# A gated mix of full and local attention on one core: projections, folds and spare matmuls on 32-column strips, local products moved to GpSimd

## The chip, the cores and the metric

One NeuronCore of a Trainium2 chip runs the whole kernel; the other cores are idle. The metric is the device time of one execution in microseconds (us). In this text PE is TensorE, ACT is ScalarE, DVE is VectorE, POOL is GpSimd and SP is SyncE, the names that the profile uses.

## The reference

Two attentions over the same input, mixed by a gate for each position, in bfloat16:

```python
x = A_x                                       # 1 x 2048 x 640, 32 heads of 20
g = sigmoid((x * gate_w).sum(-1, keepdims=True))
a = full attention: q, k, v = split(x @ A_wqkv); softmax(q @ k.T * 20**-0.5) @ v; @ A_wo
b = local attention: q, k, v = split(x @ B_wqkv); position s looks at s, s-2, ..., s-14
    (8 positions, those below 0 masked), softmax over the 8, weighted sum of v; @ B_wo
out = g * a + (1 - g) * b
```

The full attention has 32 x 2048 x 2048 exponentials, and that is where the time goes.

## The kernel before, in words

**Units and steps.** The scores are cut into units of 128 keys x 512 queries of one head: 4 chunks of queries x 8 quads of heads x 16 blocks of keys x 4 heads of a quad = 2048 units. A group is one chunk and one quad (64 units). A step is what ScalarE exponentiates with one instruction (`mk_exp`, L1377): two or three units that lie side by side in PSUM, in banks 0 to 2 and 3 to 4 by turns, where bank 5 joins the second when it is free. TensorE makes the scores of a step in `mk_qk` (L1319; heads are 32 rows of the array each), and multiplies the exponentials with the values in `mk_pv` (L1411; the output of each of four heads is a strip of 32 columns of the array, so four run side by side). Bank 6 gathers a group's sum; when it is done, `gen_norm` transposes and divides it on VectorE.

**Units of VectorE.** Some units never reach ScalarE. The lanes `gen_xm`, `gen_xr` and `gen_x` take a unit into bank 5 or 7, or in place of the third unit of a step (`xstep`, which has to meet a deadline with a margin, `XMARG`). VectorE copies it out as scaled 16-bit integers (L1566), and for every two units three instructions (L1596, L1600, L1604) make two bfloat16 parts of the exponential out of the bits. Both parts go to L1411, so that such a unit costs TensorE two of its matmuls.

**Projections and folds.** `gen_k`, `gen_q`, `gen_v`, `gen_F` and `gen_V` project x to keys, queries and values through `chain` and `mm_part` (L503) and `v_chunk` (L614), with matmuls of 128 x 128 weights; `q_fin` (L714) adds a bound that takes the place of the softmax's maximum. `gen_fold` and `gen_prefold` multiply the finished attention outputs by the output weights, also by L503, and `a_half` (L862) and `l_pre` (L896) do so at the end. `spare` (L1914, L1919, L1929) puts matmuls without use into idle time of TensorE: it does so when the planner's share of busy time in the last 3413 ns falls below `SPW`.

**The local attention.** For each of 4 chunks of 512 positions: `gen_F` makes q and k, multiplies them on VectorE (L1016) and sums over a head with a matmul against `Sel` (L992, strips of 32 columns). `gen_K` makes the softmax over the 8 positions on VectorE, and then, for each block of 128 positions, TensorE transposes the weights into strips, VectorE copies them to `attnT` (L1123), and four products of two window positions each follow on VectorE, 1280 elements for each partition. The first (L1150) writes to `accs`; the other three (L1160) write to one of `NTM` = 2 buffers `tmps`, and each is added to `accs` by two accumulating DMAs, one for each window position, which GpSimd issues (L1162). The second buffers of both kinds lie in parts of x that are dead by then (`xT`). When all have landed, VectorE adds the two halves of `accs` (L1177), and the fold of the chunk can take them.

**What sets the order.** The order of instructions on every engine is fixed when the kernel is built. A planner (`_Sched.task` and the loop at the end of `_build`) keeps a clock for every engine, with a cost for every instruction, and emits steps one after the other; between two steps it asks the lanes (`ready`) whether their next instruction fits before TensorE's next scores are due. 20 constants steer it, `BASE_`, or an entry of `SEG` for each stretch of 24 steps: among them `SPW`, `XMARG`, the least number of units that a group keeps for the other lanes, and `LW`, the local work that VectorE ought to have done by the end. On the chip each engine runs its own list in order and waits with semaphores where a task depends on another engine's.

Of the kernel before, what the change touches and what calls it, by code (L numbers as in the profile page):

```python
# [6 lines left out]
BF16 = mybir.dt.bfloat16  # L7
# [43 lines left out]
BASE_ = (0.65, 500.0, 28, 4, 10, 12, 315000.0, 1, 0.0, 1, 1.0, 40, 20, 3000.0, 1e9, 3, 8, 2, -1, 200.0)  # L51
SEG = {
# [51 lines left out]
class _Sched:  # L104
# [6 lines left out]
    def __init__(self, nc, ctx):  # L111
        self.nc = nc
        self.lists = {s: [] for s in self.STREAMS}
        self.sems = {s: ctx.enter_context(nc.semaphore("s_" + s)) for s in self.STREAMS}
        self.dma_sems = {
            s: [ctx.enter_context(nc.semaphore("d_%s%d" % (s, i))) for i in range(n)]
            for s, n in self.DMA_POOL.items()
        }
        self.bufs = {}
        self.n = 0  # L120
        self.dma_final = {}
        self.clk = {s: 0.0 for s in self.STREAMS}
        self.mode = None
        self.flow = []
        self.made = []

    def task(self, stream, fn, reads=(), writes=(), dma=False, accum=(), extra=(), cost=60.0, mode="s", dlat=4000.0, flow=None):
# [34 lines left out]
        if dma:  # L162
            t.end = at + dlat
            t.fin = t.end
            self.clk[stream] = at + (860.0 if stream == "pool" else 500.0)
        else:
            if stream == "pe":
                if mode != self.mode:
                    at += self.TURN
                    self.mode = mode  # L170
                self.flow.append((at, cost if flow is None else flow))
            t.end = at + cost
# [141 lines left out]
def _build(ctx, nc, A_x, A_wqkv, A_wo, B_wqkv, B_wo, gate_w, out):  # L314
# [27 lines left out]
    attnT = sb([P, WIN * P], BF16, "attnT")  # L342
    NPR = 3
# [150 lines left out]

    bst = {b: None for b in SB}

    def mm_part(b, mms, k0, n, reads, cost):
        bst[b] = "mid" if k0 + len(mms) < n else None

        def fn(e):  # L500
            ins = None
            for k, (o, l, r) in enumerate(mms):
                ins = e.matmul(o, l, r, start=(k0 + k == 0), stop=(k0 + k == n - 1))  # L503
            return ins

        if k0 == 0:
            return T("pe", fn, reads=reads, writes=[("bk", b)], cost=cost)
        return T("pe", fn, reads=reads, accum=[("bk", b)], cost=cost)
# [83 lines left out]
    def chain(b, mms, reads, w=1.0, cost=MM):  # L592
        n = len(mms)
        for k, m in enumerate(mms):
            yield ("pe", cost, w)
# [11 lines left out]
    def v_chunk(b, p, gi, kb, i_):  # L607
# [3 lines left out]
        def fn(e):  # L611
            ins = None
            for c in range(CN):
                ins = e.matmul(bank[b][:, i_ * wn:(i_ + 1) * wn], xT[:, kb // 4, c, (kb % 4) * P:(kb % 4 + 1) * P],  # L614
                               WvA[:, c, w0:w0 + wn], start=(c == 0), stop=(c == CN - 1))
# [3 lines left out]
        if i_ == 0:  # L619
            T("pe", fn, reads=rd, writes=[("bk", b)], cost=375)  # L620
        else:
            T("pe", fn, reads=rd, accum=[("bk", b)], cost=375)
# [25 lines left out]
    def gen_v(p, g0=0):  # L648
        for gi in range(g0, 6):
            b = yield from take(True)  # L650
            lo, hi = VG[gi]
            for i_, kb in enumerate(range(lo, hi)):
                yield ("pe", 375.0, 1.0)
# [36 lines left out]
    def gen_q(gi):  # L690
# [12 lines left out]
        yield ("pe", MM, 1.0)  # L703
# [9 lines left out]
    def q_fin(b, gi, q):  # L713
        T("pe", lambda e: e.matmul(bank[b], KM[:, q, :], qabs_hi, start=False, stop=True, skip_group_check=True),  # L714
          reads=["qabs", ("KM", q)], accum=[("bk", b)], cost=MM)
# [39 lines left out]
    def gen_norm(gi):  # L755
# [16 lines left out]
        for a, z in zip(cut, cut[1:]):  # L772
# [3 lines left out]
            if gi < HG:  # L776
                yield ("dve", 170.0 + 1.05 * (z - a) * m, 0.0)
            T("dve", lambda e, rg_v=rg_v, rr_b=rr_b, c=c, w=z - a: e.tensor_tensor(rgD[st][:, mo:mo + m, c:c + w], rg_v, rr_b, ALU.mult),
              reads=["rg", ("rr", i)], writes=[("rgD", st, h) for h in sorted({c // 32, (c + z - a - 1) // 32})], cost=170.0 + 1.05 * (z - a) * m)
# [79 lines left out]
    def a_half(o, blk, hf, fs, first, last, b):  # L859
        for f in fs:  # L860
            st, sp = first and f == fs[0], last and f == fs[-1]
            T("pe", lambda e, f=f, st=st, sp=sp: e.matmul(o, *a_mm(o, QCN - 1, f, blk, FW * hf)[1:], start=st, stop=sp),  # L862
              reads=[("oTh", max(0, blk - 1)) if f == CN - 1 else ("oT", (QCN - 1) % 2, f)] + w_rd(f),
              **({"writes": [("bk", b)]} if st else {"accum": [("bk", b)]}), cost=140)
# [7 lines left out]
    def gen_lfold():  # L872
        for blk in (0, 1, 2):
            for hf in range(2):
# [4 lines left out]
                yield ("pe", 280.0, 1.0)  # L879
# [13 lines left out]
    def l_pre(hf, k):  # L893
        b = l_banks()[hf]
        if k < 2:
            T("pe", lambda e: e.matmul(bank[b][:, 0:FW], ident[:, :], acch[:, k, hf, :], start=(k == 0), stop=False),  # L896
              reads=["ident", ("acch", k, hf)], **({"accum": [("bk", b)]} if k else {"writes": [("bk", b)]}), cost=140)
# [46 lines left out]
    KPC = 1480.0  # L944
    DLAT, DSLACK = 4700.0, 500.0
    tmrd = {}

    def gen_F(tc):
# [33 lines left out]
        for half in range(2):  # L982
# [20 lines left out]
            for idx in range(2 * CN):  # L1003
# [5 lines left out]
                if wq == 1 and f > 0:  # L1009
# [7 lines left out]
                      reads=["qB", "kB"], writes=[("prod", r)], cost=690)  # L1017
# [39 lines left out]
    def gen_K(tc):  # L1057
# [27 lines left out]
        T("dve", lambda e: e.tensor_tensor(M_(4), L_q(0, 4), L_q(4, 4), ALU.max), reads=["L"], writes=["aT"], cost=420)  # L1085
        yield ("dve", 290.0, 290.0)
        T("dve", lambda e: e.tensor_tensor(M_(2), M_(2), M_hi(2), ALU.max), reads=["aT"], writes=["aT"], cost=290)
        yield ("dve", 220.0, 220.0)
        T("dve", lambda e: e.tensor_tensor(mx[:, :, :], M_(1), M_hi(1), ALU.max), reads=["aT"], writes=["mx"], cost=220)
        yield ("dve", 700.0, 700.0)  # L1090
        yield after(T("dve", lambda e: e.tensor_tensor(L_4d, L_4d, mx_b, ALU.subtract), reads=["mx"], writes=["L"], cost=700))
# [6 lines left out]
        T("dve", lambda e: e.tensor_tensor(S_(0, 4), L_q(0, 4), L_q(4, 4), ALU.add), reads=["L"], writes=["aT"], cost=690)  # L1098
        yield ("dve", 430.0, 430.0)
        T("dve", lambda e: e.tensor_tensor(S_(0, 2), S_(0, 2), S_(2, 2), ALU.add), reads=["aT"], writes=["aT"], cost=430)  # L1100
        yield ("dve", 290.0, 290.0)
        T("dve", lambda e: e.tensor_tensor(sm[:, :, :], S_(0, 1), S_(1, 1), ALU.add), reads=["aT"], writes=["sm"], cost=290)
# [4 lines left out]
        T("dve", lambda e, gBb=gBb: e.tensor_tensor(sm[:, :, :], sm[:, :, :], gBb, ALU.mult), reads=["gB"], writes=["sm"], cost=280)  # L1107
        T("dve", lambda e: e.tensor_tensor(A_4d, A_4d, sm_b, ALU.mult), reads=["sm"], writes=["L"], cost=1225)
# [990 lines left out]
```

## Time and profile before

| what | value |
|---|---|
| median of 3 runs | 864.42 us (864.2 to 864.7) |
| the profiled execution | 865.48 us, of which the span from first to last instruction is 863.7 |
| mean granted TensorE clock | 0.987 |
| instructions | 16606; TensorE 6862 matmuls and as many weight loads |
| busy | TensorE 798.3 us, VectorE 716.9, ScalarE 839.3, GpSimd 87.3 |
| exponentials on ScalarE (L1377) | 755 instructions, 826.3 us |
| units on VectorE (L1566) | 232 |
| local products on VectorE (L1150, L1160) | 16 and 48, about 1.48 us each |
| accumulating DMAs issued by GpSimd (L1162) | 96, 84.2 us; 3.7 to 4.5 us to landing |

A row of the page's groups reads: line, engine, operation, output <- input, count | busy time, mean length of one in ns | idle time of the engine just before, and what ended it. A row of the stretches table reads: stretch, its length, then for PE, PEld (weight loads), DVE, ACT and POOL the busy time and in brackets the number of instructions, then the granted clock, the share of the DMA engines and GB/s. A row of a timeline reads: start, length, engine, line, operation, names, count, and in square brackets the idle time ahead of it and who ended that.

### The profile page before, as it was taken

The page shows a single profiled execution, that of the slowest core. Times are in us where ns is not written, and L with a number is a line of the kernel's source. Part 1 is how long each engine was busy: PE and PEld are TensorE (multiplying, and loading weights), DVE is VectorE, ACT ScalarE, POOL GpSimd, SP SyncE. Part 2 cuts the span into 40 slices and gives each one's busy share as a digit, 9 for nine tenths or more (in the row PEclk, how much of TensorE's full clock was granted, in tenths as well). Part 3 has the DMA queues.
Part 4 walks back from the last instruction along what each step waited for, and adds up shares of the span by engine and source line. Part 5 has one row for each costly group of instructions (what it writes and reads, how often), then busy time and mean ns, then how long its engine had stood idle before and what let it go on. Part 6 is the DMA issues. An engine that isn't in the chain of part 4 may idle for free.

```text
span 863.7 us, 16606 instructions
## 1 busy us (share of the span) xinstructions
PE 798.3 (92%) x6862; PEld 246.9 (29%) x6862; DVE 716.9 (83%) x1303; ACT 839.3 (97%) x781; POOL 87.3 (10%) x103
## 2 busy tenths in 40 slices
PE   9999999999999999988999999998998999788996
PEld 6322332223333222222232222322122232222233
DVE  6586867878777779888888998998699898999885
ACT  6999999999999999999999999999799999999997
POOL 1000000000000022022222210033020000332000
PEclk9999999999999999999999999999699999999999
DMA  8233011011010175378456631198260011886000
GB/s 184 45 50 52 6 25 8 3 29 8 4 10 6 38 109 105 41 119 128 68 106 98 111 60 38 19 181 127 32 104 5 10 13 25 138 129 108 1 2 32
DMA packets 141311, 51.30 MB, mean 59 GB/s; under 512 B 120628, under 2 KB 128948, under 8 KB 141236
## 3 DMA queue, kind: packets, MB, share of 16 engines
q0 software_dynamic: 13824, 31.46, 21.7%
q1 hardware_dynamic: 126612, 18.59, 14.1%
q8 instruction: 54, 0.88, 0.4%
q10 hardware_dynamic: 800, 0.18, 0.1%
q14 instruction: 21, 0.17, 0.1%
HBM read 16.14 MB, written 2.62 MB: 22 GB/s over the span
## 4 chain that ended last, share of the span: by engine, by line
ACT 84%; DMA 6%; PE 5%; DVE 3%; issue 1%; POOL 0%; SPq 0%; DVEq 0%
ACT ebuf L1377 84%; DMA accW<-tmps 3%; DMA accW<-xT 2%; PE ps L1319 2%; PE ps L503 1%; PE ps L1411 1%; DVE tmps L1160 1%; DVE accW L1150 1%; PE ps L1229 1%; DMA x_tm<-in_A_x_dram 1%; PE ps L1205 0%; ACT L_sb L1093 0%; DVE xt L1566 0%; POOL accW L1162 0%; DVE attnT L1123 0%
## 5 line engine op out<-in xcount | busy, mean ns | idle before, releaser
L1377 ACT ACTIVATE ebuf<-ps 128x1536 bf16<-128x1536 f32 (+1 forms) x755 | 826.3, 1412 | 11.3 <-PE ps L1319 11.3
L1319 PE MATMUL ps<-qT,kT 32*128 32x512 bf16 x1984 | 297.6, 388 | 51.6 <-ACT ebuf L1377 38.5
L1411 PE MATMUL ps<-ebuf,vA 128*21 128x512 bf16 (+2 forms) x1926 | 208.2, 374 | 0.5 <-DVE vA L632 0.4
L1566 DVE TENSOR_SCALAR xt<-ps 128x512 int16<-128x512 f32 x232 | 157.5, 685 | 52.9 <-PE ps L1319 51.2
L1319 PEld LDWEIGHTS ps<-qT,kT 32*128 32x128 bf16 x1984 | 72.0, 91 | 328.0 <-ACT ebuf L1377 281.2
L1162 POOL DMA_DIRECT2D accW<-tmps x36 | 31.6, 952 | 550.5 <-DVE rr L768 311.9
L1604 DVE TENSOR_TENSOR xw<-xt,xw 128x1024 bf16<-128x1024 bf16 x116 | 79.1, 682 | 1.6
L503 PE MATMUL ps<-xT,WqkB 128*128 128x512 bf16 x200 | 62.9, 390 | 1.4 <-DVE lgtr L1022 1.2
L1411 PE MATMUL ps<-xw,vA 128*21 128x512 bf16 (+2 forms) x250 | 64.1, 373 | 0.0
L1411 PEld LDWEIGHTS ps<-ebuf,vA 128*21 128x21 bf16 x1926 | 43.1, 90 | 64.0 <-issue 54.8
L1411 PE MATMUL ps<-xe,vA 128*21 128x512 bf16 (+2 forms) x250 | 59.7, 375 | 0.0
L1016 DVE TENSOR_TENSOR prod<-qk 128x1024 bf16<-128x1024 bf16 x80 | 51.9, 682 | 2.1 <-PE ps L992 1.9
L1600 DVE TENSOR_SCALAR xw<-xt 128x1024 uint16<-128x1024 uint16 x116 | 48.7, 420 | 3.9 <-PE ps L1411 3.7
L1596 DVE TENSOR_SCALAR xe<-xt 128x1024 uint16<-128x1024 uint16 x116 | 48.5, 418 | 2.6 <-PE ps L1411 1.8
L503 PE MATMUL ps<-xT,WqP 128*128 128x512 bf16 x155 | 47.8, 391 | 0.3 <-DVE xt L1566 0.2
L503 PE MATMUL ps<-xT,WkP 128*128 128x512 bf16 x140 | 41.8, 384 | 0.0
L717 DVE TENSOR_SCALAR qT<-ps 128x512 bf16<-128x512 f32 x32 | 22.1, 690 | 16.7 <-PE ps L714 16.6
L503 PE MATMUL ps<-WvA,oBacc 128*128 128x320 bf16 x160 | 32.0, 307 | 1.2 <-DVE outsb L825 1.2
L979 DVE CAST qk<-ps 128x512 bf16<-128x512 f32 x40 | 27.2, 681 | 6.6 <-PE ps L503 6.3
L614 PE MATMUL ps<-WvA,xT 128*128 128x160 bf16 (+1 forms) x320 | 30.6, 234 | 0.0
L503 PE MATMUL ps<-woA_r,oTd 128*128 128x320 bf16 x144 | 29.5, 301 | 0.0
L503 PE MATMUL ps<-xT,WvB 128*128 128x512 bf16 x100 | 29.3, 383 | 0.0
(129 smaller groups left out, 708.3 us busy)
## 6 DMA issues: line engine op xcount, KB each, us to landing
accW<-tmps POOLq DMA_DIRECT2D x36, 320.0 KB, 4.5
accW<-xT POOLq DMA_DIRECT2D x24, 320.0 KB, 4.4
xT<-xT POOLq DMA_DIRECT2D x24, 320.0 KB, 4.2
WqkB<-in_B_wqkv_dram SPq DMA_DIRECT2D x40, 160.0 KB
xT<-tmps POOLq DMA_DIRECT2D x12, 320.0 KB, 3.7
WqP<-in_A_wqkv_dram SPq DMA_DIRECT2D x135, 20.0 KB
x_tm<-in_A_x_dram SPq DMA_DIRECT2D x8, 320.0 KB
out_dram<-outsb SPq DMA_DIRECT2D x24, 80.0 KB
```

The costliest lines, as they stand in the source:

```text
L503: ins = e.matmul(o, l, r, start=(k0 + k == 0), stop=(k0 + k == n - 1))
L614: ins = e.matmul(bank[b][:, i_ * wn:(i_ + 1) * wn], xT[:, kb // 4, c, (kb % 4) * P:(kb % 4 + 1) * P], WvA[:, c, w0:w0 + wn], start=(c == 0 ...
L979: give(b, T("dve", lambda e, dst=dst, b=b: e.tensor_copy(dst, bank[b]), reads=[("bk", b)], writes=[key], cost=690))
L1016: t = T("dve", lambda e, r=r, q_ap=q_ap, k_ap=k_ap: e.tensor_tensor(prod[r][:, :, :], q_ap, k_ap, ALU.mult), reads=["qB", "kB"], writes=[( ...
L1162: tmrd[m] = [T("pool", lambda e, r=r, m=m: e.dma_start(accs[r], tmps[m][:, D * (r % 2):D * (r % 2) + D], accum_op=ALU.add), reads=[("tmps" ...
L1319: return e.matmul(o, kT[js, q, kb * P:(kb + 1) * P], qT[g % NQT][js, :], start=True, stop=True)
L1377: return T("act", lambda e: e.activation(ebuf[:, 512 * p:512 * (p + n)], ps[:, b0 * 512:(b0 + n) * 512], ACTF.Exp, scale=LN2 / ONE), reads ...
L1411: ins = e.matmul(bank[OB][32 * j:32 * j + DH + 1, o:o + w], vv, ap[:, w * i:w * i + w], start=st and i == 0, stop=sp and i == len(ks) - 1)
L1566: r = T("dve", lambda e, b=b, i=i, sl=sl: e.tensor_scalar(xt[sl][:, 512 * i:512 * i + 512].bitcast(I16), bank[b], XB, 0.0, op0=ALU.add, op ...
L1596: tx = T("dve", lambda e, r=r, t0=t0: e.tensor_scalar(xe[r][:, :].bitcast(U16), t0.bitcast(U16), 0x7F80, XMU, op0=ALU.bitwise_and, op1=ALU ...
L1600: T("dve", lambda e, r=r, t0=t0: e.tensor_scalar(xw[r][:, :].bitcast(U16), t0.bitcast(U16), 0x007F, 0x3F00, op0=ALU.bitwise_and, op1=ALU.b ...
L1604: t = T("dve", lambda e, r=r, t0=t0: e.tensor_tensor(xw[r][:, :], t0, xw[r][:, :], ALU.mult), reads=tk, writes=[("xw", r)], cost=690)
```

## The change

It has four parts.

1. *Strips.* A new function issues every matmul of 128 weight columns as four of 32 columns, each into 32 partitions of the same PSUM bank, with the same streamed operand. `mm_part`, `v_chunk`, `q_fin`, `a_half`, `l_pre` and `spare` use it; the planner books them in mode "c", that of L1411. (In the planner a change of mode costs `TURN` = 105 ns.)
2. *Local products.* The four products of a block become eight, one for each window position, 640 elements for each partition, and run on GpSimd. The accumulating DMAs are as before, each issued behind its own half, and the buffer's halves have dependences of their own.
3. *A second buffer of local weights*, `attnU`: blocks take turns, `attns[bl % 2]`. The softmax's scratch use of `attnT` stays.
4. *The planner.* It keeps lists of the last instructions of VectorE and GpSimd that are marked `lock=True`, and starts none of the one engine's within one of the other's: the products on GpSimd, and on VectorE L1016, L1596, L1600, L1604, the rescaling in `gen_norm`, L1177 and the softmax's tensor-tensor instructions. Accumulating DMAs are booked as served one after the other, 1650 ns each, and their issue with 900 ns (860 before). All constants of `BASE_` and `SEG` are other ones (`SPW` mostly 0.6, from 0.65; `XMARG` mostly 80, from 500; `LW` mostly 180000, from 315000), so that everything is placed anew, 258 units as the short description says.

The core of the diff:

```diff
+    attns = [(attnT, "aT"), (sb([P, WIN * P], BF16, "attnU"), "aU")]
...
+    def cols(e, o, l, r, **kw):
+        ins = None
+        for j in range(4):
+            ins = e.matmul(o[32 * j:32 * j + 32, :], l[:, 32 * j:32 * j + 32], r, **kw)
+        return ins
...
     def mm_part(b, mms, k0, n, reads, cost):
...
-                ins = e.matmul(o, l, r, start=(k0 + k == 0), stop=(k0 + k == n - 1))
+                ins = cols(e, o, l, r, start=(k0 + k == 0), stop=(k0 + k == n - 1))
...
-        return T("pe", fn, reads=reads, accum=[("bk", b)], cost=cost)
+        return T("pe", fn, reads=reads, accum=[("bk", b)], cost=cost, mode="c")
...
         def ev_aT(bl, b):
-            return T("dve", lambda e: e.tensor_copy(attnT[:, :], bank_bf[b]), reads=[("bk", b)], writes=["aT"], cost=690)
+            aw, ak = attns[bl % 2]
+            return T("dve", lambda e: e.tensor_copy(aw[:, :], bank_bf[b]), reads=[("bk", b)], writes=[ak], cost=690)
...
-                T("dve", lambda e, vv=vv, av=av, m=m: e.tensor_tensor(tmp4[m], vv, av, ALU.mult),
-                  reads=["aT", vkey], writes=[("tmps", m)] + dead, cost=KPC)
-                tmrd[m] = [T("pool", lambda e, r=r, m=m: e.dma_start(accs[r], tmps[m][:, D * (r % 2):D * (r % 2) + D], accum_op=ALU.add),
-                             reads=[("tmps", m)], writes=[("accs", r)], dma=True, dlat=DLAT) for r in (st, st + 1)]
+                for i in range(2):
+                    av = fap(aw, aw[:, (u + i) * P:(u + i) * P + 1], [[0, CN], [1, P]])
+                    vv = fap(vB4, vB4[:, 0, off + DIL * i:off + DIL * i + 1], [[512 + PADB, CN], [1, P]])
+                    yield ("pool", KPH, KPH)
+                    if u == 0:
+                        T("pool", lambda e, vv=vv, av=av, st=st, i=i: e.tensor_tensor(acc4[st // 2][:, i, :, :], vv, av, ALU.mult),
+                          reads=[ak, vkey], writes=[("accs", st + i)] + dead, cost=KPH, lock=True)
+                        continue
+                    T("pool", lambda e, vv=vv, av=av, m=m, i=i: e.tensor_tensor(tmp4[m][:, i, :, :], vv, av, ALU.mult),
+                      reads=[ak, vkey], writes=[("tmps", m, i)] + dead, cost=KPH, lock=True)
+                    T("pool", lambda e, r=st + i, m=m, i=i: e.dma_start(accs[r], tmps[m][:, D * i:D * i + D], accum_op=ALU.add),
+                      reads=[("tmps", m, i)], writes=[("accs", st + i)], dma=True, dlat=DLAT, serve=1650.0)
...
+        if k == "pool":
+            if clk["pool"] > clk[eng] + 30.0:
+                return False
+            adv(g)
+            return ready(g, s, eng, lim)
...
-        if now + 215.0 + (sch.TURN if sch.mode != "s" else 0.0) > lim or share(now) > SPW:
+        if now + 215.0 + (sch.TURN if sch.mode != "c" else 0.0) > lim or share(now) > SPW:
...
-                T("pe", lambda e, b=b: e.matmul(bank[b], ident[:, :], xT[:, 3, 0, :], start=True, stop=True),
-                  reads=["ident", ("xT", 3)], accum=[("bk", b)], cost=215)
+                T("pe", lambda e, b=b: cols(e, bank[b], ident[:, :], xT[:, 3, 0, :], start=True, stop=True),
+                  reads=["ident", ("xT", 3)], accum=[("bk", b)], cost=215, mode="c")
```

`KPH`, the planner's cost of one product on GpSimd, is 1100 ns; `KPC`, the cost of one of VectorE's, was 1480.

More of the change, by code (lines that the diff above doesn't have):

```diff
@@ L125, in __init__, with task @@
         self.made = []
-    def task(self, stream, fn, reads=(), writes=(), dma=False, accum=(), extra=(), cost=60.0, mode="s", dlat=4000.0, flow=None):
+        self.served = 0.0
+        self.locks = {"dve": [], "pool": []}
+    def task(self, stream, fn, reads=(), writes=(), dma=False, accum=(), extra=(), cost=60.0, mode="s", dlat=4000.0, flow=None, lock=False, serve=0.0):
         deps = {}
@@ L171, in task @@
                 self.flow.append((at, cost if flow is None else flow))
+            if lock:
+                for a, z in self.locks["pool" if stream == "dve" else "dve"]:
+                    if a <= at < z:
+                        at = z
+                self.locks[stream].append((at, at + cost))
+                del self.locks[stream][:-4]
             t.end = at + cost
@@ L619, in v_chunk @@
         if i_ == 0:
-            T("pe", fn, reads=rd, writes=[("bk", b)], cost=375)
+            T("pe", fn, reads=rd, writes=[("bk", b)], cost=375, mode="c")
         else:
-            T("pe", fn, reads=rd, accum=[("bk", b)], cost=375)
+            T("pe", fn, reads=rd, accum=[("bk", b)], cost=375, mode="c")
     def v_evac(b, p, gi, eng="dve"):
@@ L713, in q_fin @@
     def q_fin(b, gi, q):
-        T("pe", lambda e: e.matmul(bank[b], KM[:, q, :], qabs_hi, start=False, stop=True, skip_group_check=True),
-          reads=["qabs", ("KM", q)], accum=[("bk", b)], cost=MM)
+        T("pe", lambda e: cols(e, bank[b], KM[:, q, :], qabs_hi, start=False, stop=True, skip_group_check=True),
+          reads=["qabs", ("KM", q)], accum=[("bk", b)], cost=MM, mode="c")
         qmade.add(gi)
@@ L778, in gen_norm @@
             T("dve", lambda e, rg_v=rg_v, rr_b=rr_b, c=c, w=z - a: e.tensor_tensor(rgD[st][:, mo:mo + m, c:c + w], rg_v, rr_b, ALU.mult),
-              reads=["rg", ("rr", i)], writes=[("rgD", st, h) for h in sorted({c // 32, (c + z - a - 1) // 32})], cost=170.0 + 1.05 * (z - a) * m)
+              reads=["rg", ("rr", i)], writes=[("rgD", st, h) for h in sorted({c // 32, (c + z - a - 1) // 32})], cost=170.0 + 1.05 * (z - a) * m, lock=True)
         for f in range(CN):
@@ L895, in l_pre @@
         if k < 2:
-            T("pe", lambda e: e.matmul(bank[b][:, 0:FW], ident[:, :], acch[:, k, hf, :], start=(k == 0), stop=False),
-              reads=["ident", ("acch", k, hf)], **({"accum": [("bk", b)]} if k else {"writes": [("bk", b)]}), cost=140)
+            T("pe", lambda e: cols(e, bank[b][:, 0:FW], ident[:, :], acch[:, k, hf, :], start=(k == 0), stop=False),
+              reads=["ident", ("acch", k, hf)], **({"accum": [("bk", b)]} if k else {"writes": [("bk", b)]}), cost=140, mode="c")
         else:
@@ L1016, in gen_F @@
                 t = T("dve", lambda e, r=r, q_ap=q_ap, k_ap=k_ap: e.tensor_tensor(prod[r][:, :, :], q_ap, k_ap, ALU.mult),
-                      reads=["qB", "kB"], writes=[("prod", r)], cost=690)
+                      reads=["qB", "kB"], writes=[("prod", r)], cost=690, lock=True)
             yield after(t)
@@ L1148, in gen_K @@
                         dead = [("xT", 1)] if st else []
-                    yield ("dve", KPC, KPC)
-                    T("dve", lambda e, vv=vv, av=av, st=st: e.tensor_tensor(acc4[st // 2], vv, av, ALU.mult),
-                      reads=["aT", vkey], writes=[("accs", st), ("accs", st + 1)] + dead, cost=KPC)
-                    continue
-                m = tmctr[0] % NTM if tc > 0 or dead0() else 0
-                tmctr[0] += 1
-                for t in tmrd.get(m, []):
-                    yield after(t)
@@ L1177, in gen_K @@
                 T("dve", lambda e, acc=acc, fs=fs: e.tensor_tensor(acc, acc3[fs], acc3[fs + 1], ALU.add),
-                  reads=[("accs", fs), ("accs", fs + 1)], writes=[("oBacc", fb)], cost=822)
+                  reads=[("accs", fs), ("accs", fs + 1)], writes=[("oBacc", fb)], cost=822, lock=True)
                 if tc > 0 and bl < 3:
@@ L1597, in gen_x @@
                                                                 op1=ALU.bitwise_or),
-                   reads=tk, writes=[("xe", r)], cost=XTS)
+                   reads=tk, writes=[("xe", r)], cost=XTS, lock=True)
             yield ("dve", XTS, 0.0)
@@ L1601, in gen_x @@
                                                            op1=ALU.bitwise_or),
[L1602 removed]
+              reads=tk, writes=[("xw", r)], cost=XTS, lock=True)
             yield ("dve", 690.0, 0.0)
             t = T("dve", lambda e, r=r, t0=t0: e.tensor_tensor(xw[r][:, :], t0, xw[r][:, :], ALU.mult),
[L1605 removed]
+                  reads=tk, writes=[("xw", r)], cost=690, lock=True)
             xcred[0] -= 1
@@ L1918, in spare @@
         if cnt[0] + xcnt_[0] > 0:
-            T("pe", lambda e: e.matmul(bank[OB], ident[:, :], zrow, start=False, stop=False, skip_group_check=True),
-              reads=["ident", "zt"], accum=[("ob", j) for j in range(4)], cost=215)
+            T("pe", lambda e: cols(e, bank[OB], ident[:, :], zrow, start=False, stop=False, skip_group_check=True),
+              reads=["ident", "zt"], accum=[("ob", j) for j in range(4)], cost=215, mode="c")
             spares[0] += 1
```

70 lines of the change are left out of this document (37 added, 33 removed), and 52 rows, old and new, of the table SEG.

## The prediction

> **What bounds the kernel now.** I read the page's busy table and slices first, then ScalarE's groups with shapes kept apart, the waits, the table by stretches, and last the timelines of VectorE and TensorE around the one stretch where ScalarE falters.
>
> ```profile
> span 863.7 us, 16606 instructions
> ...
> PE 798.3 (92%) x6862; PEld 246.9 (29%) x6862; DVE 716.9 (83%) x1303; ACT 839.3 (97%) x781; POOL 87.3 (10%) x103
> ...
> PEclk9999999999999999999999999999699999999999
> ...
> ACT 84%; DMA 6%; PE 5%; DVE 3%; issue 1%; POOL 0%; SPq 0%; DVEq 0%
> ```
>
> ScalarE is busy 839.3 of 863.7 us. TensorE's 92% are modelled ends of pipelined matmuls; it mostly waits for ScalarE, as the waits show next. The granted clock has one dip.
>
> ```profile
> L1377 ACT ACTIVATE ebuf<-ps 128x1024 bf16<-128x1024 f32 x449 | 512.0, 1240 | 7.9 <-PE ps L1319 7.9
> L1377 ACT ACTIVATE ebuf<-ps 128x1536 bf16<-128x1536 f32 x306 | 509.5, 1665 | 3.4 <-PE ps L1319 3.4
> ...
> PEld ps L1319 <- ACT ebuf L1377: 281.2, 593, 1.4
> ...
> ACT ebuf L1377 <- PE ps L1319: 11.3, 19, 0.9
> ...
> DVE tmps L1160 <- DMA accW<-tmps: 8.2, 6, 2.3
> ```
>
> The first two lines are ScalarE's exponentials: 449 of two score units, 306 of three, so 898 + 918 = 1816 units of the 2048. The missing 232 are the L1566 instructions, where VectorE makes the exponential. Both shapes together are busy 826.3 us (group for line 1377 on the page), 0.455 us a unit at this mix; a third unit in a step adds 1665 - 1240 = 425 ns. ScalarE stands still before exponentials for only 11.3 us. TensorE's score matmuls wait 281.2 us for ScalarE. So the end is set by how many units ScalarE gets, plus its few stalls.
>
> ```profile
> 550.00:600.00 50.00, 46.65 (x428) 13.81 (x424) 45.61 (x71) 50.00 (x46) 13.76 (x16) 1.00 0.74 122
> 600.00:620.00 20.00, 18.55 (x87) 3.22 (x87) 13.81 (x26) 14.44 (x15) 2.08 (x3) 0.57 0.38 66
> ...
> 596.80 0.42 DVE L1600 TENSOR_SCALAR xw<-xt 128x1024 uint16<-128x1024 uint16 x1
> 599.30 1.49 DVE L1160 TENSOR_TENSOR tmps<-vB,attnT 128x1280 f32<-128x1280 bf16 x1 [2.08 <-DMA accW<-tmps]
> 600.71 0.68 DVE L1566 TENSOR_SCALAR xt<-ps 128x512 int16<-128x512 f32 x1
> ...
> 599.23 0.39 PE L1319 MATMUL ps<-qT,kT 32*128 32x512 bf16 x2
> 601.45 0.63 PE L1319 MATMUL ps<-qT,kT 32*128 32x512 bf16 x4 [1.83 <-ACT ebuf L1377]
> ```
>
> These explain half the stalls. At 597.2 VectorE comes to a local product (L1160) whose buffer is still read by an accumulating DMA, and stands for 2.08 us. The copy out of PSUM queued behind it (L1566) is late, TensorE starts nothing from 599.24 to 601.45, its clock falls to 0.57 in the mean over 600 to 620, and ScalarE is busy 14.44 of 20 us, after 50.00 of 50 before. That one wait costs 5.6 us there and 0.2 just after: 5.8 us.
>
> **The change, part by part.** *Units on ScalarE.* I read "258 units placed anew" as VectorE's units, 129 pairs where there are 116. ScalarE then has 26 fewer: 26 x 0.425 = 11.1 us if steps only get narrower, 26 x 0.455 = 11.8 at the same mix; I take **-11.8**. The mix is open: a step costs (826.3 - 1816 x 0.425) / 755 = 0.072 us beside its units; at 2.5 units a step rather than 1816 / 755 = 2.41 there are 28 steps fewer, 2.0 us, and I allow as much the other way.
>
> *Does VectorE have the time?* The local products leave it: 48 of L1160 (70.8 us) and 16 of L1150 (23.8), 94.6 us. A unit costs L1566's 685 ns plus half of L1596, L1600 and L1604 (418 + 420 + 682), 1.445 us; 26 are 37.6 us. VectorE goes from 716.9 to about 660, before any waiting for GpSimd, so the cover is there.
>
> *Products on GpSimd.* 128 halves of 640 elements, and 96 accumulating DMAs as now (36 + 24 + 24 + 12), each for one half. No row shows a GpSimd product. Its nearest rows are IOTA, 160 elements in 270 ns, which gives 1.08 us for 640; below stands half of VectorE's own product, 0.74; above, the strided MEMSET of 512 in 2.44, which gives 3.05. I take 1.1, IOTA's value and also the diff's planning cost; that planner's other costs match their rows (690 for 685, 420 for 418, 1480 for 1478). So 141 us of products, and 84.2 us of DMA issue as now (31.6 + 21.2 + 21.1 + 10.3). The products run in four stretches (308 to 408, 417 to 509, 553 to 645, 724 to 799: 359 us), where GpSimd would be 63% busy; at 1.85 us a product it would be 89%, at 3.05 late by 115 us. Below 1.85 nothing here is on the path.
>
> The Trainium skill ("GPSIMD Engine Reference", Performance versus the Vector engine) gives a two-input operation on 2048 elements as 4497 ns, so 1405 for 640 by estimate. By it the products take 39 us more, still beside other work; no row here shows it.
>
> *Where the stall goes.* The wait for a free product buffer moves to GpSimd's queue. Behind it there stand the next half and its DMA, and who waits for these are VectorE's add L1177, the copy of the local weights two blocks later (two buffers give it that distance), and the fold. VectorE keeps only L1177's wait for DMAs (2.9 us now). The 5.8 us go: **-5.8**. The other stalls, 11.3 - 5.8 - 0.8 at the very first step = 4.7, stay.
>
> *New stalls.* Products on GpSimd now run beside VectorE's instructions and may hold them up, and a static order can be wrong about it. Nothing in this trace prices that: below zero is excluded, since a second reader frees nothing; at the top stands rival A. I take as much as remains, **+4.7**, since VectorE waits for one more in-order partner.
>
> *Strips.* 1417 matmuls (899 on L503, 320 on L614, 32 on L714, 146 spares, 20 in the last fold) become four each: 4251 more matmuls and as many weight loads. Four strips of 512 columns start 219 to 222 ns after the last four (L1411 at 596.38, 596.60, 596.82), a whole one 216 (L503 at 592.515, 592.731, 592.947): 8 ns at most x 1417 = +11 us of TensorE. Projections then have the shape of the L1411 matmuls. A change of shape costs 95 to 100 ns (starts 311 to 317 apart in place of 216), and 165 such changes, counted in the starts, go: -16 us. TensorE gains some 5 us off the path (it has 281 us of waiting): 0. Both ends, +11 and -16, vanish in that wait too. The 8502 instructions more have to be fetched; today's 16606 take queue q8 0.4% of the DMA engines' span (0.88 MB), so I add nothing.
>
> *The planner's constants.* They move work without adding any; the margin ahead of a deadline goes from mostly 500 to 80 ns. That is in the new stalls.
>
> Sum: -11.8 - 5.8 + 4.7 = **-12.9 us**. The profiled execution lies at 865.48 (863.7 span, 1.8 around it), 1.1 above the median of 864.42; from that, **851.5**.
>
> **The rivals.** *A, slower: VectorE and GpSimd hold each other up.* Place: the four local stretches. VectorE is busy 311.8 of 350 us there (windows 320:410, 430:500, 550:640, 700:800), 94% in the last. Each hold-up of VectorE delays L1566 behind it, as at 599. Price: 5.8 us for a gap of 2.2 us on TensorE. For it: a product of 1.1 us is longer than nearly all of VectorE's instructions, and 80 ns of margin covers no collision; POOL's DMA issue already varies, 859 to 1241 ns. Against: the VectorE work that the diff's planner won't place beside a product (its lock lists) is about 297 us (196 for 129 pairs, 52 of L1016, some 49 of small ones), 34% of the span; with products at 141 / 359 = 39% the two fit into 73% even if never together. With one drop per stretch: 851.5 + 4 x 5.8 = 874.7. It decides from the third drop on (two give 863.1, three 868.9). Chance 0.20.
>
> The Trainium skill ("SBUF — State Buffer", Who interferes with whom) states this as an exclusive lock: the instruction that starts second waits for the whole of the first, if VectorE has two SBUF inputs or a two-port mode and GpSimd reads SBUF. By that rule every meeting costs a wait; this trace has no GpSimd product, so no run shows it yet.
>
> *B, more than forecast.* All steady stalls go (10.5 us, not 5.8) and no new ones come: 864.4 - 11.8 - 10.5 = 842.1; 840 with 28 steps fewer. For it: another 1.8 us of ScalarE's stalls (three, 409.5 to 414.8) follow VectorE's waits of 1.40 and 1.31 us at 404.5 and 406.6. Chance 0.18.
>
> *C, the 258 are no new share.* The units stay at 232 and only the stall goes: 864.4 - 5.8 + 4.7 = 863.3. Against: 232 is an even count of pairs, as 258 is, and freed VectorE time asks for use. Chance 0.07 (0.02 faster, 0.04 same, 0.01 slower).
>
> **How the numbers follow.** The forecast has 0.55. Faster: 0.55 + 0.18 + 0.02 = 0.75; same 0.04; slower 0.20 + 0.01 = 0.21. The bound of 0.2%, 1.7 us, is about what a measurement here can tell from no change. The range reaches down to B (840) and up to three clock drops of A (869); some 0.06 lies below and 0.12 above. The forecast's own range is 845 to 858: the mix (2.0) and new stalls from zero to twice 4.7.
>
> **What would show it.** L1566 258 times, and 1790 units in the two shapes of L1377, busy about 814 us; L1160 and L1150 gone from VectorE, 128 products on POOL near 1.1 us; ScalarE's idle before L1377 near 10 us; no clock below 1.00 between 550 and 650; VectorE's products (L1604, L1016) still near 682 ns. Wrong if L1604 or L1566 swell, if PEclk dips in three or more local stretches, if POOL's products pass 1.85 us, or if L1566 counts 232.

## The result, and the profile after

The change makes the kernel slower: 910.54 us (median of 4 runs, 903.8 to 912.88) against 864.31; ratio 1.0522, 95% interval 1.0462 to 1.0583. The profiled execution took 903.8 us, the fastest of the four. In the changed file the exponentials are line 1395 (1377 before), the scores 1337 (1319), VectorE's units 1584 (1566) with 1614, 1618 and 1622 (1596, 1600, 1604), the products for the logits 1032 (1016), the local products 1175 and 1178, their DMAs 1180.

The same rows of the page as before:

```profile
span 902.0 us, 25116 instructions
...
PE 805.3 (89%) x11036; PEld 262.1 (29%) x11037; DVE 769.2 (85%) x1304; ACT 833.7 (92%) x782; POOL 264.3 (29%) x231
...
PEclk9999999999999998989999879989988999896998
...
ACT 60%; DVE 21%; PE 13%; POOL 3%; issue 2%; DMA 1%; POOLq 0%; DVEq 0%
```

ScalarE has less to do, as meant, but VectorE, now without local products, is busy 52 us longer than before, the clock dips again and again from the 16th of the 40 slices on, and 21% of the chain that ended last now runs through VectorE. The groups, shapes kept apart, show where that comes from:

```profile
L1395 ACT ACTIVATE ebuf<-ps 128x1024 bf16<-128x1024 f32 x476 | 505.8, 1173 | 25.2 <-PE ps L1337 24.6
L1395 ACT ACTIVATE ebuf<-ps 128x1536 bf16<-128x1536 f32 x279 | 441.8, 1584 | 30.1 <-PE ps L1337 27.7 <-PE ps L1340 2.3
...
L1584 DVE TENSOR_SCALAR xt<-ps 128x512 int16<-128x512 f32 x258 | 174.5, 684 | 44.4 <-PE ps L1337 41.6 <-PE ps L1340 0.6
L1622 DVE TENSOR_TENSOR xw<-xt,xw 128x1024 bf16<-128x1024 bf16 x129 | 122.7, 951 | 1.9
L1618 DVE TENSOR_SCALAR xw<-xt 128x1024 uint16<-128x1024 uint16 x129 | 77.3, 599 | 8.3 <-PE ps L1429 8.2
L1614 DVE TENSOR_SCALAR xe<-xt 128x1024 uint16<-128x1024 uint16 x129 | 74.5, 578 | 4.6 <-PE ps L1429 3.7
L1032 DVE TENSOR_TENSOR prod<-qk 128x1024 bf16<-128x1024 bf16 x80 | 74.4, 960 | 2.3 <-PE ps L1008 2.1
...
L1178 POOL TENSOR_TENSOR tmps<-vB,attnT 128x640 f32<-128x640 bf16 x16 | 25.9, 1618 | 0.0
```

ScalarE stands still before exponentials for 25.2 and 30.1 us in the two shapes, 55.4 us by the page's group, where it was 11.3. Of VectorE's lines shown, the four that read and write SBUF only have swollen: lines 1622 and 1032 from 682 to 951 and 960 ns, lines 1614 and 1618 from 418 and 420 to 578 and 599. Line 1584, which reads PSUM, has not (684). A product on GpSimd takes 1556 ns in the mean over all 128 (1286 the shortest), not 1100. The stretches table (busy times of PE, PEld, DVE, ACT, POOL, then the granted clock) ties the loss to GpSimd:

```profile
250.00:300.00 50.00, 47.75 (x733) 15.55 (x727) 37.25 (x68) 50.00 (x48) 0.00 (x0) 1.00 0.19 34
...
350.00:400.00 50.00, 41.13 (x445) 10.67 (x443) 46.84 (x61) 41.51 (x38) 26.05 (x23) 0.86 0.52 92
...
650.00:700.00 50.00, 41.20 (x455) 10.10 (x450) 48.63 (x72) 42.25 (x41) 21.95 (x19) 0.90 0.45 66
```

From 20 us to the first product, at 314, ScalarE is busy all the time; in the two stretches with products shown here it loses 8.5 and 7.8 us of 50. The timeline shows one hold-up being passed on:

```profile
347.38 1.60 POOL L1178 TENSOR_TENSOR xT<-vB,attnU 128x640 f32<-128x640 bf16 x1
347.39 2.14 DVE L1032 TENSOR_TENSOR prod<-qk 128x1024 bf16<-128x1024 bf16 x1
...
349.46 2.61 DVE L1622 TENSOR_TENSOR xw<-xt,xw 128x1024 bf16<-128x1024 bf16 x1
...
349.88 1.63 POOL L1178 TENSOR_TENSOR tmps<-vB,attnU 128x640 f32<-128x640 bf16 x1
...
351.99 2.83 DVE L1032 TENSOR_TENSOR prod<-qk 128x1024 bf16<-128x1024 bf16 x2
...
352.66 1.60 POOL L1178 TENSOR_TENSOR tmps<-vB,attnU 128x640 f32<-128x640 bf16 x1
...
354.74 0.68 DVE L1063 CAST vB4b<-ps 128x512 bf16<-128x512 f32 x1
...
355.47 0.62 PE L507 MATMUL ps<-xT,WvB 128*32 128x512 bf16 x4 [2.35 <-DVE vB4b L1063]
...
356.81 1.45 ACT L1395 ACTIVATE ebuf<-ps 128x1536 bf16<-128x1536 f32 x1 [3.17 <-PE ps L1337]
```

Line 1032 starts with a product and ends at 349.53, 0.55 us after the product's end at 348.98, though it needs 0.68 by itself. Line 1622 is held in the same way until the next product has ended at 351.51, and the two of line 1032 behind it until a third has, at 354.26. The PSUM copies queued behind (1063, 1584) come late, TensorE stands 2.35 us, ScalarE 3.17, and the clock falls (0.86 in this stretch of 50 us).

The whole trace has the same pattern. Of lines 1622 and 1032, which need 0.68 us, 25 started inside a product as recorded, and 24 of them ended 0.55 or 0.56 us after its end. Of lines 1614 and 1618, which need 0.42, 38 did, and all ended 0.28 or 0.29 after it. Both fit an instruction that does nothing beside the product and starts 0.13 us before the product's recorded end. Another way to be slowed by a product, a semaphore wait for its result or its DMA, is small: the waits of other engines for these add up to 3.9 us (two waits of line 1057).

### The profile page after: what moved, and what is told of

It reads as the page before. It is cut to its first block, busy times and chain, and to the rows that moved or that the text cites. A ratio compares the mean times of both kernels' runs of the same rounds, so it can differ in the third digit from the quotient of the medians.

```text
span 902.0 us, 25116 instructions
## 1 busy us (share of the span) xinstructions
PE 805.3 (89%) x11036; PEld 262.1 (29%) x11037; DVE 769.2 (85%) x1304; ACT 833.7 (92%) x782; POOL 264.3 (29%) x231
## 4 chain that ended last, share of the span: by engine, by line
ACT 60%; DVE 21%; PE 13%; POOL 3%; issue 2%; DMA 1%; POOLq 0%; DVEq 0%
ACT ebuf L1395 60%; DVE prod L1032 4%; PE ps L1337 4%; PE ps L507 4%; DVE xw L1622 3%; DVE xt L1584 3%; PE ps L1429 3%; DVE xw L1618 3%; DVE xe L1614 2%; POOL xT L1178 1%; DVE qT L732 1%; PE ps L1223 1%; DMA accW<-tmps 1%; PE ps L1247 1%; DVE rgD L793 1%
## 5 line engine op out<-in xcount | busy, mean ns | idle before, releaser
L1395 ACT ACTIVATE ebuf<-ps 128x1536 bf16<-128x1536 f32 (+1 forms) x756 | 820.5, 1324 | 55.4 <-PE ps L1337 52.3
L1622 DVE TENSOR_TENSOR xw<-xt,xw 128x1024 bf16<-128x1024 bf16 x129 | 122.7, 951 | 1.9
L1175 POOL TENSOR_TENSOR accW<-vB,attnT 128x640 f32<-128x640 bf16 x8 | 11.7, 1480 | 351.0 <-DVE attnT L1140 351.0
L1618 DVE TENSOR_SCALAR xw<-xt 128x1024 uint16<-128x1024 uint16 x129 | 77.3, 599 | 8.3 <-PE ps L1429 8.2
L1614 DVE TENSOR_SCALAR xe<-xt 128x1024 uint16<-128x1024 uint16 x129 | 74.5, 578 | 4.6 <-PE ps L1429 3.7
L1032 DVE TENSOR_TENSOR prod<-qk 128x1024 bf16<-128x1024 bf16 x80 | 74.4, 960 | 2.3 <-PE ps L1008 2.1
L507 PE MATMUL ps<-xT,WqkB 128*32 128x512 bf16 x800 | 65.6, 382 | 0.7 <-DVE qk L995 0.7
L507 PE MATMUL ps<-xT,WqP 128*32 128x512 bf16 x620 | 50.2, 395 | 2.9 <-DVE xt L1584 2.9
L507 PE MATMUL ps<-xT,WkP 128*32 128x512 bf16 x560 | 45.8, 382 | 0.0
L507 PE MATMUL ps<-woA_r,oTd 128*32 128x320 bf16 x640 | 39.6, 309 | 2.2 <-DVE oTd L800 2.2
L507 PE MATMUL ps<-WvA,oBacc 128*32 128x320 bf16 x640 | 35.6, 309 | 0.8 <-DVE qk L995 0.5
L507 PE MATMUL ps<-xT,WvB 128*32 128x512 bf16 x400 | 33.5, 401 | 3.0 <-DVE vB4b L1063 2.3
```

Of the source, the lines that this page charges most:

```text
L507: ins = e.matmul(o[32 * j:32 * j + 32, :], l[:, 32 * j:32 * j + 32], r, **kw)
L1032: t = T("dve", lambda e, r=r, q_ap=q_ap, k_ap=k_ap: e.tensor_tensor(prod[r][:, :, :], q_ap, k_ap, ALU.mult), reads=["qB", "kB"], writes=[( ...
L1175: T("pool", lambda e, vv=vv, av=av, st=st, i=i: e.tensor_tensor(acc4[st // 2][:, i, :, :], vv, av, ALU.mult), reads=[ak, vkey], writes=[(" ...
L1395: return T("act", lambda e: e.activation(ebuf[:, 512 * p:512 * (p + n)], ps[:, b0 * 512:(b0 + n) * 512], ACTF.Exp, scale=LN2 / ONE), reads ...
L1614: tx = T("dve", lambda e, r=r, t0=t0: e.tensor_scalar(xe[r][:, :].bitcast(U16), t0.bitcast(U16), 0x7F80, XMU, op0=ALU.bitwise_and, op1=ALU ...
L1618: T("dve", lambda e, r=r, t0=t0: e.tensor_scalar(xw[r][:, :].bitcast(U16), t0.bitcast(U16), 0x007F, 0x3F00, op0=ALU.bitwise_and, op1=ALU.b ...
```

## The experiments

Theory L: VectorE's instructions of the lock lists (those that the planner won't start within a product) stand still until a running product has ended, and products come where the plan doesn't have them. Rivals: S, the strips cost TensorE more than thought; M, the new order is fragile by itself. Later L was split: L1, the plan has a wrong length; L2, nothing on the chip holds a product to its planned place. "Planner's clock" is the kernel's own bookkeeping, no time of the chip.

**e1_short: the same order, small products.**

```diff
-    av = fap(aw, ..., [[0, CN], [1, P]])      # 640 elements
+    av = fap(aw, ..., [[0, CN], [1, 8]])      # 40; vv and the outputs likewise
```

> The changed kernel with every engine's order kept instruction for instruction; only each product on GpSimd works on 40 of its 640 elements (8 columns of each of 5 blocks of 128), so most of the local sums is left out. Theory L (VectorE's instructions with two SBUF inputs or in a fast mode stand still until a running product has ended, and products of 1.6 us come where the planner had 1.1): with products well under 0.5 us the collisions shrink to almost nothing, the time falls to 846 to 858 us, VectorE's lines 1614, 1618 and 1622 are back at 418, 420 and 682 ns, the clock at 0.98 or more. Theory S (the strips, with 4174 matmuls and weight loads more, make TensorE late): 895 or more. Theory M (the new order with margins of 80 ns is fragile by itself): 885 or more.

Measured: 845.03 us, ratio 0.9777 (0.9736 to 0.9817).

```profile
PE 771.5 (92%) x11037; PEld 258.5 (31%) x11037; DVE 668.0 (79%) x1304; ACT 826.5 (98%) x782; POOL 135.7 (16%) x233
...
PEclk9999999999999999999999999999999999999999
...
L1625 DVE TENSOR_TENSOR xw<-xt,xw 128x1024 bf16<-128x1024 bf16 x129 | 88.2, 684 | 1.9
L1617 DVE TENSOR_SCALAR xe<-xt 128x1024 uint16<-128x1024 uint16 x129 | 54.0, 419 | 4.0 <-PE ps L1432 3.1
```

These are rows of the page and VectorE's groups of e1. But for two clearing instructions of GpSimd at the start, the instructions and their order are those of the changed kernel, and it runs 65 us faster: S and M fall, and L stands. The loss goes with the length of the products.

**e2_whole: the same order, no strips.** `cols` issues one matmul of 128 columns.

> The changed kernel with every engine's order kept; only the strips are undone, each group of four 32-column matmuls is one matmul of 128 columns again. Theory L: no gain, 900 to 920 us. Theory S: it falls to below 870. Theory M: 900 to 920 as L.

Measured: 916.14 us, 1.0591 (1.0554 to 1.0628). No gain from undoing the strips; S falls a second time.

**e3_true: measured lengths in the plan.**

```diff
-    KPH = 1100.0
+    KPH = 1600.0        # and 540 ns to the DMA, 600 from its start to the next product
```

> The changed kernel planned with what its trace shows of GpSimd: 1600 ns for a product (1100 before), 540 ns from its end to its DMA, 600 ns from the start of a DMA's issue to the next product; all placed anew with the same constants. The planner's own clock then ends at 857.0 us, with 248 units on VectorE, where it ended at 823.1 with 258; before the change it ended at 834.3. Theory L, collisions from the wrong length: fewer of them, 880 to 895, still above before, since 23 us of it are planned. Theory M: 905 or more, as the margins are the same.

Measured: 896.67 us, 1.0386 (1.033 to 1.0443), 2 us above the expected stretch. Lines 1614, 1618 and 1622 have become 1616, 1620 and 1624, and in its groups are as long as ever (628, 645 and 905 ns). The right length alone did not keep the two engines apart; L1 had to be doubted.

**e4_dveprod: the products back on VectorE**, in halves, all else as changed and placed anew (`T("pool", ...)` is `T("dve", ...)`, 815 ns planned).

> The changed kernel with the products back on VectorE, in halves (815 ns planned for one); strips, second buffer of local weights, constants and the planner's other rules as changed, all placed anew. The planner's clock ends at 844.5 us with 220 units on VectorE, 10 more than for the kernel before. Theory L: 870 to 880, the planner's difference to before and little else. Theory S or M: 890 or more, since strips and margins are all there.

Measured: 867.37 us, 1.0033 (1.0019 to 1.0046), below the expected stretch. VectorE's lines are back at 418, 417 and 685 ns. With 12 units fewer on VectorE than before the change, which by the prediction's 0.425 us a unit are worth 5.1 us, the kernel is only 3 us slower: the rest of the change, as placed here, shows no cost of its own.

**e5_half: the same order, products of 320 elements** (as e1, 64 columns of each block).

> The changed kernel with every engine's order kept; each product works on 320 of its 640 elements (half of the local sums is left out). By the first runs 40 elements take about 0.59 us and 640 about 1.56, so 320 should take 1.04 us, the 1.1 that the planner had. Theory L1 (the collisions come from the wrong length of a product): almost none are left, 846 to 856 us. Theory L2 (no wait on the chip holds a product to its planned place, GpSimd runs free between its semaphores, so products and VectorE's instructions meet by chance whatever the planned length): collisions shrink about with the product's length, 862 to 885 us, lines 1614, 1618 and 1622 still 15 to 40% longer than 418, 420 and 682 ns.

Measured: 857.98 us, 0.9927 (0.9901 to 0.9953), between the two stretches. Products took 994 ns in the mean, so the plan's 1100 was kept (though with its DMA one came every 2.19 us, where the plan has 2.0), and still lines 1614 and 1618 had 519 and 500 ns in their new places, line 1622 had 823. VectorE lost half of what it lost to whole products (the sums stand behind e12), as L2 has it, but the kernel is only 13 us slower than e1, a fifth of the 65. That short hold-ups are caught up before ScalarE needs the next scores would explain it; no run shows this by itself.

**e6_write: GpSimd writes, and reads nothing.**

```diff
-    e.tensor_tensor(tmp4[m][:, i, :, :], vv, av, ALU.mult)
+    e.iota(tmp4[m][:, i, :, :].bitcast(I32), [[P, CN], [1, P]], base=0, channel_multiplier=1)
```

> The changed kernel with every engine's order kept; in place of a product GpSimd writes 640 counted-up numbers (an iota, about 0.95 us by the page's row of 160 in 270 ns), reading nothing: all local products are left out. If VectorE is held up only by a GpSimd instruction that reads SBUF: line 1622 and line 1032 at 682 ns, lines 1614 and 1618 at 418 and 420, 843 to 850 us, as with the 40 elements. If writing holds up as well: lines 1614 and 1618 longer by 15 to 40%, 855 to 885 us, as with half products of the same length.

Measured: 850.08 us, 0.9831 (0.98 to 0.9863). VectorE's groups of e6:

```profile
L1626 DVE TENSOR_TENSOR xw<-xt,xw 128x1024 bf16<-128x1024 bf16 x129 | 88.2, 684 | 1.9
L1618 DVE TENSOR_SCALAR xe<-xt 128x1024 uint16<-128x1024 uint16 x129 | 68.7, 533 | 4.5 <-PE ps L1433 3.6
L1622 DVE TENSOR_SCALAR xw<-xt 128x1024 uint16<-128x1024 uint16 x129 | 65.2, 505 | 9.6 <-PE ps L1433 9.5
L1036 DVE TENSOR_TENSOR prod<-qk 128x1024 bf16<-128x1024 bf16 x80 | 52.1, 683 | 3.7 <-PE ps L1012 3.4
```

Neither expectation fits whole. VectorE's two products with two SBUF inputs (1626, 1036 here) run free beside a GpSimd instruction that only writes; the two fast integer instructions (1618, 1622 here) are held up by it, 27 and 20% longer. Beside e5's products of nearly the same length (994 against 888 ns) all four were held up.

**e7_held: measured lengths, and products that wait.**

```diff
+        if lock and stream == "pool":
+            add(self.lastlock)      # the last VectorE instruction of the lock lists placed ahead
```

> The kernel of e3 (planned with GpSimd's measured lengths), and every product waits with a semaphore for the last VectorE instruction of the lock lists planned ahead of it, so that GpSimd can't run ahead of its place; placed anew, nothing left out. The planner's clock ends at 859.4 us with 248 units, 2.4 later than e3. Theory L2: fewer collisions than e3's, 876 to 889 us (the planner's end and the 23 us that lay between plan and chip with the products on VectorE). Theory L1: no better than e3, 892 to 905. Either way slower than before the change, since the plan itself is 25 us longer.

Measured: 877.18 us, 1.0154 (1.0125 to 1.0182), as L2 had it. The chip is 18 us behind the plan, where e3 was 40 behind.

**e8_dve_placed: products on VectorE, placed for it.** Whole products of 1480 ns, strips and the booking of DMAs as changed, the 20 constants of each stretch searched anew by the planner's own clock.

> Products on VectorE whole, as in the kernel before (1480 ns planned), with the strips and with accumulating DMAs booked one after the other as in the change; the planner's constants searched anew for this kernel, its clock ends at 826.7 us with 250 units on VectorE. Theory L: nothing on GpSimd can hold VectorE up, so plan and chip lie 20 to 27 us apart as for e4 (867.4 against 844.5): 846 to 854 us. If the constants with margins of 80 ns are fragile by themselves (theory M): 860 or more.

Measured: **847.83 us**, 0.9822 (0.9787 to 0.9858). All of the local sums are there, and this is faster than both kernels, by 1.8% of the time before.

**e9_held_placed: e7, placed for it.** The same search with the products on GpSimd and held.

> The kernel of e7 (products on GpSimd, planned with their measured lengths, each waiting for the VectorE instruction planned ahead of it) with constants searched anew for it; the planner's clock ends at 828.8 us with 248 units on VectorE. Theory L2: plan and chip 18 to 24 us apart as for e7 (877.2 against 859.4): 847 to 853 us, faster than the kernel before. If holding works only where the plan is loose: 860 or more.

Measured: 849.98 us, 0.9838 (0.9809 to 0.9867). All of the local sums are there too. A row of GpSimd's timeline in e9 shows a wait at work:

```profile
341.75 0.88 POOL L1193 DMA_DIRECT2D accW<-tmps  x1 [0.56 <-POOL tmps L1191]
343.55 1.40 POOL L1191 TENSOR_TENSOR tmps<-vB,attnU 128x640 f32<-128x640 bf16 x1 [0.92 <-DVE xe L1627]
```

The product stood 0.92 us until VectorE's line 1627 had ended.

**e10_dve_whole: e8 without strips**, in the same order.

> The kernel of e8 with every engine's order kept and each group of four strips one matmul of 128 columns again. If strips are worth the changes of shape that they save (95 to 100 ns each): 1 to 8 us slower than e8. If four weight loads and matmuls cost more than they save: faster than e8.

Measured: 849.49 us, 0.9829 (0.9801 to 0.9857). The medians differ by 1.7 us the expected way, but the intervals overlap almost wholly: no worth of the strips could be measured. e10 has whole matmuls and products on VectorE from one buffer of local weights, like the kernel before, and differs from it in the planner's bookings and constants alone. So these are worth the 14 us between the two (863.89 was measured beside e10), and the move to GpSimd, even with waits (e9), gains nothing over products on VectorE (e8). Which of the bookings and constants does it was not taken apart.

**e11_unheld: e9 without the waits**, same order and plan (`lastlock` counts in the planner's times and is no dependence).

> The kernel of e9 with every engine's order and plan kept; only the waits are left out that hold a product until the VectorE instruction planned ahead of it has ended (the data's own waits stay). Theory L2 (GpSimd runs ahead of its planned place and meets VectorE by chance): 870 to 900 us, VectorE's lines of the lock lists longer by a third or more in the mean, as in e3. Theory L1 (measured lengths in the plan are enough): 847 to 856, as e9.

Measured: 905.98 us, 1.0474 (1.0428 to 1.052). Its groups of VectorE and its waits:

```profile
L1635 DVE TENSOR_TENSOR xw<-xt,xw 128x1024 bf16<-128x1024 bf16 x124 | 122.4, 987 | 2.1
L1627 DVE TENSOR_SCALAR xe<-xt 128x1024 uint16<-128x1024 uint16 x124 | 80.8, 652 | 6.5 <-PE ps L1442 5.4
...
ACT ebuf L1408 <- PE ps L1350: 51.4, 54, 3.7
```

In e9 these two lines have 748 and 486 ns, and ScalarE waits 2.1 us before exponentials (0.8 + 1.3). The waits alone, at the same order and with the right lengths, are worth 56 us. The order that the planner places tasks in, set beside the traces, shows what they prevent: in e11 101 of the 128 products started before the last VectorE instruction of the lock lists placed ahead of them had ended, up to 10.6 us before, and the plan has none; in e9 none did. That settles L2.

**e12_after_held: the changed kernel with the waits added**, same order, 1100 ns still in the plan.

> The changed kernel with every engine's order kept and the wrong lengths still in the plan (1100 ns); only the waits are added that hold a product until the last VectorE instruction of the lock lists placed ahead of it has ended. If running ahead is most of the loss: 860 to 885 us. If the wrong lengths are: 895 to 915, since products planned back to back still run late into VectorE's next instructions.

Measured: 881.04 us, 1.0185 (1.0151 to 1.0219). Of the 46 us that the change lost, the waits give back 29; of the 65 that long products cost (e1), that is a little under half. Right lengths in the plan beside the waits (e7) give back 4 more. Constants searched for such products (e9) give 27 more, which ends 14 below the kernel before; how much of the 27 is the constants by themselves, and how much that they fit the lengths, was not taken apart.

Counted in the traces: in the changed kernel 16 of 128 products meet no tensor-tensor instruction of VectorE and none of lines 1614 and 1618, in e9 44, in e11 14. Of VectorE's unit and logit instructions (lines 1614, 1618, 1622, 1032 and their counterparts) the time above 420 and 683 ns adds up to 100 us in the changed kernel, 91 in e3, 104 in e11, 75 in e12, 52 in e5, 34 in e9, 1 in e1. So the waits don't end all meetings: they hold a product behind VectorE's instruction, and no semaphore holds VectorE's next one behind the product. In e9 the 34 us that are left hardly reach ScalarE, which waits the 2.1 us named above.

## Why the prediction was wrong

**The units: right.** 258 units on VectorE, 1790 on ScalarE. In e1, where nothing holds it up, ScalarE is busy 826.5 us, 12.8 less than before; the term was 11.8. In the changed kernel it is only 5.6 less: exponentials that follow each other overlap, and those that wait do so less (the lengths add up to 254 us more than the busy time in e1, to 180 in the changed kernel).

**The stall that goes: right.** VectorE no longer waits for a DMA ahead of a product, and e1's steady idle time is about 3 us: 12.8 + 8.0 (11.3 - 3.3) = 20.8 of the 21.0 us between the spans 863.7 and 842.7. The term was 5.8; the other steady stalls, which were to stay, went in part as well. The prediction without its new stalls, 863.7 - 17.6 = 846.1, missed e1's span by 3.4.

**The products: mis-sized.** 1.1 us was taken, 1.56 measured, and one every 2.74 us (median) with its DMA rather than the 2.0 that the diff's plan has. The row of IOTA was no neighbour: it reads nothing. That the diff's other costs match their rows was no evidence for this one, which had no row. The Trainium skill's figure ("GPSIMD Engine Reference", Performance versus the Vector engine), 1405 ns by estimate, was nearer; the shortest products took 1.29, those close behind a DMA's issue 1.60.

**New stalls: the step that failed.** +4.7 was taken; 902.0 - 842.7 = 59.3 us were measured between the changed kernel and the same order with small products. Rival A was the case, in its place and by its mechanism, but its price of 874.7 was far too low too: it counted one clock drop in each of four stretches, and the drops come one after the other (granted clock 0.950 over the span). What I held against A was that the two engines' work fits into 73% "even if never together", and that the planner keeps it apart. The sum was not the fault: e9 does fit it in. (Its 34% is a share of the whole span; in the four local stretches of the kernel before, the VectorE work in question takes 100 of 359 us, 28%.) But a plan in which two engines don't meet is not a wait. On the chip GpSimd starts a product as soon as its data is there: the plan of the changed kernel has one of the 128 products start before the last VectorE instruction of the lock lists placed ahead of it has ended; in the trace 59 did, the earliest 7.9 us before. e11 against e9 shows that waits can be worth 56 us, more than the 46 that the change lost. In the changed kernel itself they give back 29 of the 65 us that lie between its median and e1's (e12). The rest is not taken apart. The wrong length alone was not the cause: in e3, planned with the right one and without waits, VectorE's instructions are lengthened nearly as much (91 us in all) as in the changed kernel (100).

The rule of the Trainium skill that I cited beside A ("SBUF — State Buffer", Who interferes with whom) is what the traces show: a held instruction waits for the whole of the other, not for a share. e6 agrees also in the finer part, that an instruction with two SBUF inputs is held only against a GpSimd instruction that reads (684 and 683 ns beside the one that writes), and one in a fast mode against any (533 and 505); I take the integer instructions for such, which need 418 ns for 1024 elements where the others need 682. I gave A 0.20 with the rule at hand; it should have made every meeting a cost, and asked what prevents a meeting.

**Strips: right.** Neither e2 nor e10 shows a cost or a worth beyond its interval. **Rivals B and C** did not occur, though e1's 845.0 shows that this order without the hold-ups comes near B's 842.1.

## What to carry to other kernels

A schedule written out by hand that keeps two engines off a shared resource holds only as far as semaphores enforce it: where instructions of two engines exclude each other, give the one that can wait a dependence on the other, as for data. Before an operation is moved to a slower engine that excludes the old one, compare what it occupies with what it frees: two products of 1.56 us can hold VectorE off for 3.1 us, and spare it one of 1.48. Even with the waits the move gained nothing here over products on VectorE. And a cost that no row of the trace shows is worth one run by itself before a plan is built on it.

## What the runs showed of the hardware that was not expected

A product's length follows 0.17 us + 1.74 ns an element (shortest of 40, 320 and 640 elements: 242, 729 and 1286 ns). The 80 products of the changed kernel that start while the DMA issue before them on GpSimd still runs take 1.60 us in the median. From a product's end to the issue of its own DMA 0.54 us pass (median).

VectorE instructions that started up to 0.5 us ahead of a product's recorded start were mostly held as well: of lines 1622 and 1032 in the changed kernel 20 of 23 (line 1622 at 349.46 above is one). The other three took their usual time, and their products 1.69 to 1.79 us. In e9, where 21 of these started up to 0.2 us ahead of a product, only one was held. So the recorded starts don't tell which of the two waits when they lie this close, and why that differs is open.
